# Weight rows on a 256-byte boundary in SBUF, and text V ahead of the scores, in a two-stream attention block

## Chip, cores, metric

One core of one Trainium2 chip. The metric is device time in microseconds (us) of one execution. Executions that are not over 1.5% above the fastest of the same kernel are called fast, the others slow. Ratios are of fast runs alone; medians and ranges take in all runs. SBUF is the core's on-chip memory, HBM the large memory from which the weights come; TensorE, VectorE (DVE in the lines) and ScalarE are engines of the core.

## The reference, cut to what matters

```python
B, Ni, Nt, D = (2, 256, 32, 1152)                     # bf16
mod_i = (silu(c) @ wmod_img).reshape(B, 6, 1, D)      # shift, scale, gate: blocks 0, 1, 2 (the rest unused)
hi = layernorm(x_img) * (1 + sci) + shi               # the same for the text stream
qi, ki, vi = split(hi @ wqkv_img)                     # and qt, kt, vt
p = softmax(concat(qt, qi) @ concat(kt, ki).T * D ** -0.5)
a = p @ concat(vt, vi)
out_i = x_img + gai * (ai @ wo_img)                   # and out_t
```

Fourteen weight blocks of 1152 x 1152 bf16 (2592 KB each) are used once each. Together with the inputs, and with the gate rows that the kernel writes out and reads back, they are 39.5 MB read from HBM.

## The kernel before

Five SBUF slots of 9 x 1152 bf16 per partition hold the weights. All loads go through one queue in the order of use; a load waits until the slot's last reader is done. A row of a weight block is 2304 bytes in one partition.

```python
const = ctx.enter_context(tc.tile_pool(name="const", bufs=1))
wpool = ctx.enter_context(tc.tile_pool(name="w", bufs=1))
act = ctx.enter_context(tc.tile_pool(name="act", bufs=1))
# ...
w_v_t = load_w(1, wqkv_txt, 2 * D)
w_ga_i = load_w(3, wmod_img, 2 * D)      # image gate
w_ga_t = load_w(2, wmod_txt, 2 * D)      # text gate
w_o_i = load_w(0, wo_img, 0)
w_o_t = load_w(1, wo_txt, 0)
# ... layer norm, V of the image, shift, Q and K of the image, the text's Q and K between them ...
def img_gate():
    mod_rows(w_ga_i, 1)                  # 36 matmuls on the gate's weights, copy, write to HBM
    for b in range(B):
        nc.gpsimd.dma_start(gb[:, b, :], gsc[1, b, :].partition_broadcast(P))
# ...
img_gate()
scores_txt()
scores_img(0)
scores_img(1)
v_txt()
p_transposes(0)
txt_gate()
attn_out(0, 0, 5)
# ... p_transposes(1), the rest of attention, then the four output tiles and the text's ...
```

Matmuls and the steps wrapped in `pin` keep the order in which they are written; other steps of VectorE and ScalarE may be reordered when the program is built.

## Time and profile before

| | before |
|---|---|
| median of 3 runs | 128.75 us (127.72 to 129.01) |
| span of the profiled execution | 127.2 us |
| TensorE busy | 116.3 us (91%) |
| weights streaming | about 3 to 103 us, at 390 GB/s |

The rows of busy tenths cut the span into 40 slices of 3.2 us; a 9 means 90% busy or more. PEclk is the granted clock of TensorE, in tenths of full speed. The view of waits says which engine waited, for whom, how long in all, how often, and the longest. The timeline gives start and duration of groups of instructions, with the idle time just before a group and what ended it in brackets. Those lines are in the prediction. One more place of this trace is needed later. VectorE, between the end of the scores and attention:

```profile
93.61 0.35 DVE L493 TENSOR_SCALAR pb<-e,rs 128x256 bf16<-128x256 f32 x1
93.88 0.23 DVE L495 TENSOR_SCALAR pb<-e,rs 128x32 bf16<-128x32 f32 x1
94.02 1.85 DVE L437 TENSOR_TENSOR v_t<-ps,svb 64x288 bf16<-64x288 f32 x4
95.91 0.61 DVE L535 COPY pT<-pT_ps 128x864 bf16<-128x864 bf16 x1
```

The last softmax tile (L493, L495) ends, then text V's four subtractions run, and only then comes the copy of P transposed that attention's first matmul needs.

### The profile page before, as it was taken

Reading aid. Unit: us, or ns where it says so; the run is one execution under the profiler, and the core shown is the slowest. Engines: PE = TensorE matmul, PEld = TensorE weight load, DVE = VectorE, ACT = ScalarE, POOL = GpSimd, SP = SyncE. Lnnn points to the kernel's source line nnn. Section 1 sums busy time; section 2 is a strip of 40 time slices with the busy share of each in tenths; the row PEclk is TensorE's granted clock in tenths of the full one; section 3 lists DMA queues with packets and bytes.
Section 4 is the critical chain, followed back from the end, with each engine's and each line's share of the span. In section 5 each row is a group of like instructions: output and inputs, shape, how many; then the busy total and the mean of one; then the engine's idle time right before and its main releaser. Section 6 shows DMA issues by size and latency. Waiting matters only on the chain.

```text
span 127.2 us, 2681 instructions
## 1 busy us (share of the span) xinstructions
PE 116.3 (91%) x1144; PEld 69.0 (54%) x1154; DVE 56.1 (44%) x151; ACT 34.1 (27%) x72; POOL 14.3 (11%) x36
## 2 busy tenths in 40 slices
PE   6998799999599999999999999669998999999990
PEld 2356644454176444545448466245786776566770
DVE  1576590067702732012261221204887565566672
ACT  4799400056511113211102011113513850000000
POOL 7230000000002133000000000003214171000000
PEclk9999999999999999999999999986999999999999
DMA  4999999999999999999999999999999992202212
GB/s 119 382 374 388 399 387 394 391 393 395 358 365 392 387 394 391 349 387 392 388 393 392 388 391 389 389 392 393 393 387 385 392 298 74 93 0 93 98 46 93
DMA packets 18694, 41.03 MB, mean 323 GB/s; under 512 B 1027, under 2 KB 1563, under 8 KB 18683
## 3 DMA queue, kind: packets, MB, share of 16 engines
q1 hardware_dynamic: 17584, 39.56, 84.4%
q0 software_dynamic: 704, 1.05, 2.5%
q10 hardware_dynamic: 395, 0.26, 0.7%
q8 instruction: 9, 0.15, 0.5%
q14 instruction: 2, 0.02, 0.0%
HBM read 39.52 MB, written 1.34 MB: 321 GB/s over the span
## 4 chain that ended last, share of the span: by engine, by line
PE 45%; DMA 36%; SPq 8%; DVE 6%; issue 1%; ACT 1%; DVEq 0%; ACTq 0%
PE ps L60 31%; DMA t<-in_wqkv_img_dram 18%; DMA t<-in_wmod_img_dram 18%; PE aps L60 5%; PE gps L60 4%; SPq L87 4%; PE sps L60 3%; SPq L101 2%; PE vps L60 2%; SPq L99 2%; DVE v_t L437 1%; ACT e L489 1%; DVE nmx L486 1%; DVE pb L493 1%; DVE pb L495 1%
## 5 line engine op out<-in xcount | busy, mean ns | idle before, releaser
L60 PE MATMUL ps<-xT_i,t 128*128 128x512 bf16 x156 | 35.5, 379 | 2.1 <-DMA t<-in_wqkv_img_dram 1.5
L60 PEld LDWEIGHTS <-t 128*128 128x128 bf16 x432 | 23.1, 97 | 20.7 <-DMA t<-in_wqkv_img_dram 2.0
L60 PE MATMUL ps<-t,aT 128*128 128x384 bf16 (+3 forms) x153 | 20.2, 308 | 0.0
L60 PEld LDWEIGHTS <-aT 128*128 128x128 bf16 (+1 forms) x153 | 13.0, 101 | 7.1 <-issue 0.5
L60 PE MATMUL vps<-t,hS_i 128*128 128x512 bf16 x70 | 15.9, 379 | 0.8 <-DVE hS_i L220 0.7
L60 PEld LDWEIGHTS <-hS_i 128*128 128x128 bf16 x72 | 6.9, 98 | 8.5 <-DVE hS_i L220 0.8
L60 PE MATMUL wps<-warm 128*128 128x512 bf16 x27 | 8.9, 486 | 1.3 <-DVE warm L119 1.2
L577 DVE TENSOR_TENSOR tmp<-ps,gb 128x384 bf16<-128x384 f32 (+2 forms) x13 | 6.8, 526 | 6.3 <-PE ps L60 6.3
L153 DVE CAST v_i<-vps 128x512 bf16<-128x512 f32 x5 | 3.4, 689 | 11.6 <-PE vps L60 11.6
L60 PE MATMUL gps<-t,sT 128*32 128x256 bf16 (+1 forms) x180 | 6.2, 281 | 2.5 <-DMA t<-in_wmod_img_dram 2.4
L155 ACT CAST qkT<-ps 128x512 bf16<-128x512 f32 (+1 forms) x6 | 3.4, 569 | 18.3 <-PE ps L60 18.3
L340 DVE TENSOR_SCALAR qkT<-ps 128x512 bf16<-128x512 f32 (+1 forms) x5 | 3.3, 665 | 10.6 <-PE ps L60 10.6
L153 DVE CAST qkT<-ps 128x512 bf16<-128x512 f32 (+1 forms) x5 | 3.1, 625 | 10.7 <-PE ps L60 10.6
L342 ACT ACTIVATE qkT<-ps 128x512 bf16<-128x512 f32 (+1 forms) x6 | 3.3, 553 | 15.9 <-PE ps L60 15.9
L60 PE MATMUL aps<-pT,v_i 128*128 128x288 bf16 x36 | 6.7, 287 | 0.5 <-DVE pT L535 0.5
L449 POOL DMA_DIRECT2D mod_scratch<-g_sb x4 | 2.3, 586 | 41.9 <-ACT g_sb L155 37.3
L60 PEld LDWEIGHTS <-sT 128*32 128x32 bf16 x180 | 4.5, 96 | 4.6 <-DMA t<-in_wmod_img_dram 2.9
L60 PE MATMUL sps<-qkT 128*128 128x288 bf16 (+1 forms) x54 | 6.9, 363 | 0.0
L549 DVE TENSOR_SCALAR aT<-aps,sv_i 128x288 bf16<-128x288 f32 x9 | 4.7, 517 | 3.0 <-PE aps L60 3.0
L551 ACT ACTIVATE aT<-aps,sv_i 128x288 bf16<-128x288 f32 x9 | 4.5, 501 | 5.4 <-PE aps L60 5.4
L60 PEld LDWEIGHTS <-warm 128*128 128x128 bf16 x29 | 3.1, 116 | 5.2 <-issue 2.7
L60 PEld LDWEIGHTS <-qkT 128*128 128x128 bf16 (+1 forms) x54 | 4.6, 120 | 2.1 <-issue 0.5
(100 smaller groups left out, 113.4 us busy)
## 6 DMA issues: line engine op xcount, KB each, us to landing
t<-in_wmod_txt_dram SPq DMA_DIRECT2D x3, 2592.0 KB, 21.2
t<-in_wqkv_txt_dram SPq DMA_DIRECT2D x3, 2592.0 KB, 16.2
t<-in_wmod_img_dram SPq DMA_DIRECT2D x2, 2592.0 KB, 21.8
t<-in_wqkv_img_dram SPq DMA_DIRECT2D x2, 2592.0 KB, 24.1
t<-in_wo_img_dram SPq DMA_DIRECT2D x1, 2592.0 KB, 21.3
t<-in_wo_txt_dram SPq DMA_DIRECT2D x1, 2592.0 KB, 12.2
t<-in_wmod_img_dram SPq DMA_DIRECT2D x2, 1152.0 KB, 9.5
t<-in_wqkv_img_dram SPq DMA_DIRECT2D x2, 864.0 KB, 15.2
```

What stands on the lines that cost most here:

```text
L60: return pin(nc.tensor.matmul(*a, **k))
L87: nc.sync.dma_start(t[:, :, o:o + n], sv[:, :, o:o + n])
L99: nc.sync.dma_start(w_sc_i[:, r0:r1, :], sc_v[:, r0:r1, :])
L101: nc.sync.dma_start(w_v_i[:, r0:r1, :], v_v[:, r0:r1, :])
L153: nc.vector.tensor_copy(out_ap, in_ap)
L155: nc.scalar.copy(out_ap, in_ap)
L340: nc.vector.tensor_scalar_mul(out_ap, in_ap, SCALE)
L342: nc.scalar.mul(out_ap, in_ap, SCALE)
L449: nc.gpsimd.dma_start(gsc[si, b, :].rearrange("(g j) -> g j", g=NGG), g_sb[b:P:32, :])
L549: nc.vector.tensor_scalar(dst, aps[:], bias, None, op0=ALU.add)
L551: nc.scalar.activation(dst, aps[:], ACT.Identity, bias=bias)
L577: nc.vector.tensor_mul(tmp[:, 0:n], ps[:, 0:n], gb[:, b, c0:c0 + n])
```

## The change

The intent is twofold: each weight row and input row shall begin on a 256-byte boundary of its partition, and TensorE shall have text V and half of the scores to do while the image gate's weights are still on their way.

```diff
-    const = ctx.enter_context(tc.tile_pool(name="const", bufs=1))
+    lead = ctx.enter_context(tc.tile_pool(name="lead", bufs=1))
     wpool = ctx.enter_context(tc.tile_pool(name="w", bufs=1))
     act = ctx.enter_context(tc.tile_pool(name="act", bufs=1))
+    const = ctx.enter_context(tc.tile_pool(name="const", bufs=1))
@@
+    eps_row = lead.tile([P, 32], f32)
@@
-    eps_t = const.tile([P, 1], f32)
-    nc.vector.memset(eps_t[:], EPS)
+    eps_t = eps_row[:, 0:1]
+    nc.vector.memset(eps_row[:], EPS)
@@
-    img_gate()
+    v_txt()
     scores_txt()
     scores_img(0)
+    img_gate()
     scores_img(1)
-    v_txt()
     p_transposes(0)
```

(Cut: the indexing of `eps_t` in one activation.)

More of the change, by code (lines that the diff above doesn't have):

```diff
@@ L179, in ln_rstd @@
         rstd = small.tile([P, 1], f32, tag="rstd")
-        pin(nc.scalar.activation(rstd[0:np_, :], var, ACT.Ln, bias=eps_t[0:np_, :], scale=sign))
+        pin(nc.scalar.activation(rstd[0:np_, :], var, ACT.Ln, bias=eps_t[0:np_], scale=sign))
         pin(nc.scalar.activation(rstd[0:np_, :], rstd[0:np_, :], ACT.Exp, scale=-0.5))
```

## The prediction

> **What bounds the kernel now.** I read the page's rows of busy tenths first, then the waits of TensorE, then the busy time by stretches, then the transfers. The rows:
>
> ```profile
> PE   6998799999599999999999999669998999999990
> ...
> PEclk9999999999999999999999999986999999999999
> DMA  4999999999999999999999999999999992202212
> GB/s 119 382 374 388 399 387 394 391 393 395 358 365 392 387 394 391 349 387 392 388 393 392 388 391 389 389 392 393 393 387 385 392 298 74 93 0 93 98 46 93
> ```
>
> Two resources are full at once. The DMA engines stream weights at about 390 GB/s from the second slice to about 103 us. TensorE is full but for two dents: slice 11 (about 33 us) and slices 26 and 27 (about 83 to 89 us), where the granted clock falls too. After 103 us there is only TensorE, VectorE and the tail. So what can be won is in the dents. The view of waits, for TensorE in all, names them:
>
> ```profile
> PE gps L60 <- DMA t<-in_wmod_img_dram: 2.4, 1, 2.4
> ...
> PE ps L60 <- DMA t<-in_wqkv_img_dram: 1.5, 1, 1.5
> ...
> PE aps L60 <- DVE pT L535: 0.5, 1, 0.5
> ```
>
> The first is the image gate's rows waiting for their weights; the second is the first Q block waiting for its weights; the third is attention waiting for the copy of P transposed. The timeline of TensorE gives the places:
>
> ```profile
> 30.06 3.18 PE L60 MATMUL vps<-t,hS_i 128*128 128x512 bf16 x14
> 34.74 2.12 PE L60 MATMUL ps<-xT_i,t 128*128 128x512 bf16 x9 [1.50 <-DMA t<-in_wqkv_img_dram]
> ...
> 79.80 1.67 PE L60 MATMUL ps<-xT_i,t 128*128 128x512 bf16 x7
> 83.90 1.40 PE L60 MATMUL gps<-t,sT 128*32 128x288 bf16 x36 [2.42 <-DMA t<-in_wmod_img_dram]
> 85.07 6.86 PE L60 MATMUL sps<-qkT 128*32 128x288 bf16 x54
> 91.86 2.40 PE L60 MATMUL ps<-t,hT_t 128*64 128x288 bf16 x36
> 94.19 0.68 PE L63 MATMUL pT_ps<-ident,pb 128*128 128x128 bf16 x9
> 94.80 1.29 PE L60 MATMUL gps<-t,sT 128*32 128x288 bf16 x36
> 96.57 0.42 PE L60 MATMUL aps<-pT,v_i 128*128 128x288 bf16 x2 [0.49 <-DVE pT L535]
> ```
>
> The columns are start, duration, engine, line, operation, count and, in brackets, the idle time before. Between 34.7 and 81.5 us there is no wait worth naming. The stretches around the second dent (us, then PE, PEld, DVE, ACT and POOL busy, the granted clock, DMA share and GB/s):
>
> ```profile
> 81.50:83.90 2.40, 0.00 (x1) 0.00 (x1) 0.69 (x1) 0.00 (x0) 0.00 (x0) 1.00 1.04 388
> 83.90:85.30 1.40, 1.40 (x40) 1.15 (x44) 0.00 (x0) 0.00 (x0) 0.00 (x0) 0.87 1.06 392
> 85.30:86.50 1.20, 1.20 (x19) 0.58 (x12) 0.00 (x0) 0.40 (x1) 0.47 (x1) 0.50 1.06 396
> 86.50:88.60 2.10, 2.10 (x11) 1.34 (x12) 0.90 (x2) 1.02 (x3) 0.69 (x2) 0.56 1.05 390
> 88.60:90.00 1.40, 1.40 (x14) 1.13 (x12) 1.26 (x6) 0.59 (x2) 0.00 (x0) 1.00 1.06 393
> ```
>
> The wait of 2.4 us is paid twice: it is followed by about 3.4 us at half clock. Lost there: 0.13 x 1.4 + 0.50 x 1.2 + 0.44 x 2.1 = 1.7 us. The dent therefore costs 2.4 + 1.7 = 4.1 us. The 1.5 us wait at 33 us is followed by no slow clock (1.00 throughout).
>
> [...]
>
> **Part 1, alignment.** As the kernel before is built, the 3232 B of the pool of constants come first, from byte 16512 of a partition, so the weight slots start at 19744 = 77 x 256 + 32. A row is 2304 B = 9 x 256, a slot 81 x 256, so every weight row, and every input row behind them, starts 32 B past a boundary and touches ten 256 B blocks. In the new layout one 128 B tile comes first: 16512 + 128 = 16640 = 65 x 256, and each row touches nine. At 391 GB/s a row takes 2304 x 16 / 391e9 = 94.3 ns[...]: 410 GB/s (5% more)[...]. The wider memset (128 x 32 for 128 x 1) is on VectorE at 0.8 us, under 0.1 us, before the input has landed: free.
>
> What a faster stream is worth is read where TensorE waits for it. The Q weights land at 34.7 us and streaming began at about 3 us. At 410 the 31.7 us become 31.7 x 391/410 = 30.2, so they land at 33.2. But TensorE ends its V work at 30.06 + 3.18 = 33.24 us, and its beginning hangs on the layer norm and the scale matmuls, which wait only 0.2 us for a DMA. So the win is **1.4 us, and can't be much over 1.5** however fast the stream becomes. Later landings move up by 3 to 5 us, but TensorE waits for none of them after part 2.
>
> **Part 2, order.** Nothing is added: text V (36 matmuls, 2.4 us), text scores and the scores of image 0 move ahead of the gate rows. Their operands are there: text V's weights lie one transfer ahead of the gate's in the queue, so land near 83.9 - 2654 KB / 390 GB/s = 77 us, and Q and K are in SBUF. From 81.5 us TensorE has 2.4 us of text V, about 0.7 of text scores and 2.2 of image 0 scores (18 matmuls; the last 27 of the 54 ran from 88.6 to 91.9 us at full clock, 0.12 us each), so reaches the gate near 86.8, 3 us after its weights are in at the old rate. The wait of 2.4 goes, and with it the half clock: **4.1 us**.
>
> Given back: the wait for P transposed. It was 0.5 us with text V between the scores and the transposes. Now only the transposes (0.68) and the text gate rows (about 1.25) lie between the end of the scores and attention, 1.9 us, against the last softmax (before, its last VectorE step ended at 94.1, 2.3 us after the scores) and 0.6 us for the copy: 2.9 - 1.9 = 1.0 us. So 0.5 us is added, perhaps less, as text V's four subtractions (1.85 us of VectorE just ahead of that copy) have gone earlier; I take **0.4**.
>
> The sum: 4.1 - 0.4 + 1.4 = 5.1 us. 128.75 - 5.1 = 123.65; I say 123.6.
>
> **Rivals.** First, a later transfer takes the wait's place. The text gate weights follow the image gate's by one transfer of 6.8 us: 90.7 at the old rate; the stretch from 83.9 to 96.57 us holds 12.7 - 1.7 - 0.5 = 10.5 us of work at full clock, the last 1.25 of it the text gate, so TensorE wants them near 81.5 + 10.5 - 1.25 = 90.7. A tie at the old rate, free at a better one. The image output weights land near 97.5 and are wanted near 100. The output weights for text, which in the kernel before are issued only at 94.3 us since they need text V's slot, are issued over 10 us earlier. Against it stand all these margins; it would cost 0 to 1 us.
>
> Second, the broadcast gate rows come late. The gate's rows are now made some 3 us later; before, 13.6 us lay between the end of the gate matmuls (85.3) and the second broadcast landing (91.98 + 6.9 = 98.9), with 6.6 us to spare before its first reader at 105.5. Now the rows end near 88.2, the broadcast lands near 101.8, and the first reader wants it near 101. A wait of about 1 us on VectorE is possible, but six PSUM buffers hold TensorE's output and VectorE needs only about 0.9 of each 1.46 us chunk: absorbed.
>
> Third, alignment does nothing, because reading HBM, and not writing SBUF, sets 390 GB/s. Then only part 2 counts: 128.75 - 3.7 = 125.05, or up to 126 with the first rival. The two parts overlap as well: a stream 5% faster would by itself bring the image gate's weights to about 79.9 us and remove most of that dent, so the parts are not worth their separate sums.
>
> Fourth, the half clock stays in part, from another short idle stretch: up to 1.7 us back, 125.3.
>
> **Range and chances.** The best case, all of the first dent and no added wait, is 128.75 - 5.7 = 123.05; the runs of the kernel before spread from 127.72 to 129.01, so I go to 122.2 below. Alignment without effect and a small new wait give 125.4 above. Faster by over 2% means under 126.2; even the order alone passes that by 1.1 us. Faster 0.93, same 0.06, slower 0.01.
>
> **What would show it.** Right: mean DMA rate from 10 to 30 us well above 393 GB/s; the idle before the first Q matmul near zero; no idle before the gate rows and a granted clock of 1.00 from 80 to 95 us; the wait before attention's first matmul 0.5 to 1.0 us; the stretch from the first output matmul to the end unchanged at about 23.4 us. Wrong: a rate still at 391, a new wait at the text gate or the first output chunk, or a clock dip that stays.

## The result, and the profile after

| | before | after |
|---|---|---|
| median | 128.88 us (127.72 to 129.38, 4 runs) | 123.27 us (123.15 to 124.34, 4 runs) |
| ratio of fast runs | | 0.9596 (0.9512 to 0.968) |
| span of the profiled execution | 127.2 us | 122.6 us |
| TensorE busy | 116.3 us | 116.0 us |

A ratio is the mean time of one kernel's fast runs over that of the other's fast runs of the same rounds, so it is not quite the ratio of the medians. The rows of the changed kernel:

```profile
PE   5977979999999999999999999999999999999990
...
PEclk9998699999999999999999999999999999999999
DMA  4999999999999999999999999999999950411222
GB/s 120 375 388 389 408 407 410 411 412 413 410 381 399 415 400 411 397 407 410 408 413 411 410 406 413 417 399 412 414 406 405 405 200 24 144 42 54 102 48 96
```

Both old dents of TensorE are gone, and from the fifth slice on the stream runs at 397 to 417 GB/s, with one slice at 381. There is a new spot: the granted clock falls in slices 4 and 5, from about 11 to 14.5 us (0.50 between 12 and 14 us). That belongs to this execution; the other three of the four had a mean clock of 1.00 and took 123.15 to 123.34 us, this one 124.34. The place of the second dent, in the timeline of TensorE:

```profile
77.25 4.05 PE L61 MATMUL ps<-xT_i,t 128*128 128x512 bf16 x18
81.23 2.40 PE L61 MATMUL ps<-t,hT_t 128*64 128x288 bf16 x36
83.55 3.10 PE L61 MATMUL sps<-qkT 128*32 128x288 bf16 x36
86.58 1.29 PE L61 MATMUL gps<-t,sT 128*32 128x288 bf16 x36
87.80 2.38 PE L61 MATMUL sps<-qkT 128*128 128x288 bf16 x18
90.02 0.67 PE L64 MATMUL pT_ps<-ident,pb 128*128 128x128 bf16 x9
90.61 1.29 PE L61 MATMUL gps<-t,sT 128*32 128x288 bf16 x36
91.91 0.42 PE L61 MATMUL aps<-pT,v_i 128*128 128x288 bf16 x2
```

Not one bracket: TensorE waits for nothing from Q to the end. Attention's first matmul starts at once too, where I expected a wait. VectorE shows why:

```profile
91.25 0.60 DVE L537 COPY pT<-pT_ps 128x864 bf16<-128x864 bf16 x1
91.77 0.15 DVE L493 RECIPROCAL rs<-rs 128x1 f32<-128x1 f32 x1
91.96 0.35 DVE L495 TENSOR_SCALAR pb<-e,rs 128x256 bf16<-128x256 f32 x1
```

The copy (L537) stands ahead of the last tile's reciprocal and products (from 91.77 us), though it is written after them. It serves the other image's attention and needs nothing from that tile.

### The profile page after: what moved, and what is told of

Read it like the earlier page. It is cut to its first block, busy times and chain, and to the rows that moved or that the text cites. A ratio compares the mean times of both kernels' runs of the same rounds, so it can differ in the third digit from the quotient of the medians.

```text
span 122.6 us, 2691 instructions
## 1 busy us (share of the span) xinstructions
PE 116.0 (95%) x1154; PEld 69.1 (56%) x1154; DVE 56.1 (46%) x151; ACT 34.2 (28%) x72; POOL 14.4 (12%) x36
## 4 chain that ended last, share of the span: by engine, by line
PE 88%; DMA 7%; DVE 1%; SPq 1%; issue 0%; DVEq 0%
PE ps L61 50%; PE vps L61 14%; DMA t<-in_wmod_img_dram 7%; PE gps L61 6%; PE aps L61 6%; PE sps L61 4%; PE tp L64 2%; PE sc_ps L61 2%; PE wps L61 2%; PE pT_ps L64 1%; SPq L97 1%; DVE tmp L579 1%; DVE o L580 0%; PE gT L64 0%; PE tpt L64 0%
## 5 line engine op out<-in xcount | busy, mean ns | idle before, releaser
L61 PE MATMUL ps<-xT_i,t 128*128 128x512 bf16 x162 | 36.5, 379 | 0.0
L157 ACT CAST v_i<-vps 128x512 bf16<-128x512 f32 x4 | 2.3, 580 | 12.3 <-PE vps L61 12.3
L61 PE MATMUL sps<-qkT 128*128 128x288 bf16 (+1 forms) x54 | 5.5, 287 | 0.0
```

Source lines behind the costliest of these rows:

```text
L61: return pin(nc.tensor.matmul(*a, **k))
L157: nc.scalar.copy(out_ap, in_ap)
```

## The experiments

The theory after the result has five points. The rate depends on how many 256-byte blocks a row touches in SBUF (ten in the kernel before, at 392 GB/s from 20 to 30 us, nine in the changed one, at 412). A faster stream is worth 1.4 us at the first Q matmul. Either part of the change alone removes most of the wait for the gate's weights. The half clock comes from that wait. The wait for P transposed fell away through VectorE's order. All results were correct save the one that is wrong on purpose. The runs called slow, which the ratios leave out, are one of copy_last, one of before_again, and 4 of the 27, 1 of the 11 and 4 of the 18 runs of the kernel before.

| run | median us (range, runs) | before in the same rounds | ratio of fast runs |
|---|---|---|---|
| align_only | 124.04 (123.88 to 124.75, 6) | 127.88 (27) | 0.9684 |
| order_only | 124.55 (124.36 to 125.04, 6) | the same | 0.9720 |
| after_again | 123.20 (122.89 to 124.14, 6) | the same | 0.9623 |
| before_filled | 127.77 (127.48 to 128.45, 22) | the same | 0.9999 |
| offset_128 | 124.45 (124.32 to 124.64, 4) | 128.62 (11) | 0.9703 |
| offset_224 | 124.75 (124.43 to 125.06, 4) | the same | 0.9722 |
| source_32 | 122.72 (122.60 to 122.81, 4) | the same | 0.9564 |
| copy_last | 124.26 (124.04 to 126.96, 6, one slow) | the same | 0.9691 |
| before_again | 127.78 (127.18 to 129.29, 14) | 127.97 (18) | 0.9997 |
| after_third | 123.41 (123.04 to 123.90, 5) | the same | 0.9655 |
| start_filled | 123.34 (123.25 to 123.38, 4) | the same | 0.9651 |
| before_third | 127.62 (one look) | 128.61 (1) | |

### Each part alone: align_only, order_only, after_again

```diff
 align_only: the new pools, and the old order
+    img_gate(); scores_txt(); scores_img(0); scores_img(1); v_txt(); p_transposes(0)
 order_only: the old pools, and the new order
+    v_txt(); scores_txt(); scores_img(0); img_gate(); scores_img(1); p_transposes(0)
 after_again: the changed kernel, unedited
```

> The new layout with the old order of work. Theory (the two parts mend the same dent): the DMA rate is 405 to 412 GB/s as in the changed kernel, Q's weights land near 33.3 us, and the image gate's weights land near 80.4 us, when TensorE is ready for them near 79.9, so the wait of 2.4 us shrinks to 0.5 or less and no half clock follows it. The 0.5 us wait for P transposed stays. Expected 124.1 us (123.4 to 125.0), that is within 1 us of the changed kernel. Rival (each part has its own gain, alignment only that of Q's weights): 127.4 us.

> The new order with the old layout, rows 32 bytes past a boundary. Theory: the rate stays at 391 GB/s, the 1.5 us wait for Q's weights stays, the wait before the gate rows and the half clock go, and no wait for P transposed appears: 128.9 - 4.1 - 0.5 = 124.3 us (123.8 to 125.3). Rival (the text gate's or the output weights arrive too late at the old rate): a new wait of 0.5 to 1.5 us, 125.0 to 126.0. Rival (additive parts): what alignment did not give, 128.9 - 4.0 = 124.9, which this run cannot tell from the theory; the run of alignment alone can.

> The changed kernel again, for its times on the same chip as the three others. 123.2 us in runs without a slow clock in the start, some 124.3 in runs with one.

Alignment alone gave 124.04 us (124.1 expected, 127.4 by the rival). Its timeline at the two dents:

```profile
29.87 3.19 PE L61 MATMUL vps<-t,hS_i 128*128 128x512 bf16 x14
33.51 2.12 PE L61 MATMUL ps<-xT_i,t 128*128 128x512 bf16 x9 [0.46 <-DMA t<-in_wqkv_img_dram]
...
80.54 1.29 PE L61 MATMUL gps<-t,sT 128*32 128x288 bf16 x36 [0.28 <-DMA t<-in_wmod_img_dram]
81.65 5.30 PE L61 MATMUL sps<-qkT 128*32 128x288 bf16 x54
...
92.05 0.42 PE L61 MATMUL aps<-pT,v_i 128*128 128x288 bf16 x2 [0.95 <-DVE pT L537]
```

The wait for the gate's weights shrank to 0.28 us without any reordering. The wait for P transposed, of which I had expected that it stays at 0.5 us, was 0.95. So the parts are not additive: alone they are worth 3.2% and 2.8%, together 3.8%. The intervals of these ratios overlap, since the kernel before spreads so much; the runs themselves show it better: all of align_only took 123.88 us or more, all of order_only 124.36 or more, and five of the six of after_again 123.58 or less. The order alone gave 124.55 us (124.3 expected) and kept its 1.60 us wait for Q's weights. From order_only to after_again alignment is worth 124.55 - 123.20 = 1.35 us. In after_again the first Q matmul started at 33.12 us, and its last short wait was no longer for a DMA:

```profile
29.66 3.18 PE L61 MATMUL vps<-t,hS_i 128*128 128x512 bf16 x14
33.12 2.12 PE L61 MATMUL ps<-xT_i,t 128*128 128x512 bf16 x9 [0.28 <-DVE xT_i L323]
```

So there is a cap on what a faster stream can give there: VectorE's modulation of the input is the next limit. It lies close: in align_only Q still waited for its weights, 0.46 us, in start_filled 0.35, and in source_32 for VectorE again. From align_only to after_again the order is worth 0.84 us; the two waits that it removes, 0.95 us for P transposed and 0.28 for the gate, would make 1.2.

### Which bytes and which side: offset_128, offset_224, source_32

```diff
 offset_128, on the changed kernel
-    eps_row = lead.tile([P, 32], f32)
+    eps_row = lead.tile([P, 64], f32)
 offset_224
+    eps_row = lead.tile([P, 88], f32)
 source_32 (wrong result on purpose)
     def wview(src, c0):
+        if src.shape[1] > D:
+            c0 += 16 if c0 == 0 else -16
```

> The changed kernel with the leading tile 256 bytes wide in place of 128, so that every weight row starts 128 bytes past a 256-byte boundary. Theory [...]: the rate from 20 to 30 us is 391 GB/s as at offset 32, and the time is that of the order alone, 124.5 us. Rival (what counts is a boundary of 64 or 128 bytes): 410 to 412 GB/s and 123.2 us. [...]

> The same with a leading tile of 352 bytes, rows 224 bytes past a boundary. Theory of blocks: 391 GB/s again, 124.5 us. Rival of 64-byte boundaries: 391 here too but 411 at offset 128. [...]

> Wrong result on purpose: SBUF rows stay on the boundary, and the twelve loads from the wide weights read columns shifted by 16 elements, so that each row in HBM starts 32 bytes past a boundary or before one. Theory (what costs is the write into SBUF): 408 to 412 GB/s from 20 to 30 us and 123.2 us. Rival (the read [...] costs the same): 391 GB/s and 124.5 us.

The start of each row in SBUF was read from the programs as built: 32 bytes past a 256-byte boundary before, 0 in the changed kernel, 128 and 224 in these two. Busy times, granted clock, DMA share and GB/s from 20 to 30 us. Before:

```profile
20.00:30.00 10.00, 9.79 (x84) 4.91 (x85) 2.78 (x6) 1.91 (x4) 0.00 (x0) 1.00 1.05 392
```

The changed kernel:

```profile
20.00:30.00 10.00, 10.00 (x72) 4.73 (x73) 2.83 (x7) 1.76 (x3) 0.00 (x0) 1.00 1.04 412
```

offset_128:

```profile
20.00:30.00 10.00, 9.61 (x86) 4.86 (x85) 2.87 (x6) 2.00 (x4) 0.00 (x0) 1.00 1.05 391
```

offset_224:

```profile
20.00:30.00 10.00, 10.00 (x79) 4.79 (x76) 2.63 (x6) 1.76 (x3) 0.00 (x0) 1.00 1.05 391
```

source_32, aligned in SBUF and shifted in HBM:

```profile
20.00:30.00 10.00, 10.00 (x88) 4.94 (x86) 3.23 (x9) 2.56 (x5) 0.00 (x0) 1.00 1.04 412
```

The last column decides: 391 or 392 at offsets 32, 128 and 224, and 412 at 0, with the source rows in place and with them shifted by 32 bytes. Neither the size of the offset nor a boundary of 64 or 128 bytes matters in these runs, and the shift on the read side doesn't either. What the three slow layouts share is one more 256-byte block per row in SBUF, and with it two blocks that a row fills in part only. No run tells these two apart; rows whose length is no multiple of 256 bytes would. The times agree: 124.45 and 124.75 us, as with the order alone. That source_32 is some 0.5 us quicker than the changed kernel in other rounds is not explained; the changed kernel did not run in its rounds.

### Does the idle time cause the half clock: before_filled, before_again, before_third

```diff
 before_filled, on the kernel before, ahead of img_gate()
+    fps = ps_tr.tile([P, 512], f32, tag="tr")
+    for _ in range(11):
+        mm(fps[:], lhsT=warm[:, 0:P], rhs=warm[:], start=True, stop=True)
 before_again, before_third: the kernel before, unedited
```

> The kernel before with eleven matmuls of 128x512 on a zero tile ahead of the image gate's rows (11 x 0.216 = 2.4 us of work that nobody reads), so that TensorE is busy while it waits for the gate's weights. Theory (the half clock comes from the idle 2.4 us): the granted clock stays at 1.00 from 80 to 95 us and the kernel wins the 1.7 us lost at half clock: 127.2 us (126.7 to 127.8). Rival (the slow clock has another cause, such as the load of the work there): the dip stays and the time is 128.9 or more.

> The kernel before, for a second trace. Theory (the half clock behind the wait for the gate's weights comes in some executions only[...]): its runs fall in two groups, near 127.4 us and near 128.9 us, and a trace of the first group shows the same wait of about 2.4 us with a granted clock of 1.00 behind it. Rival (the wait itself is shorter in the faster executions): a wait near 1 us there.

> The kernel before, one more look, for a trace of its quicker group of executions (mean clock 1.00 or a dip in the start only, span near 125.6 us), which fell in about 6 of 10. Theory: the wait for the gate's weights is 2.0 to 2.5 us as in the slower group, and no half clock follows it, so the 54 matmuls of the scores take 5.3 us in place of 6.9. Rival: the wait is near 1 us there. If the trace falls in the slower group, this stays open.

before_filled missed its number: I expected 127.2 and it took 127.77, the same as the kernel before in its rounds. The clock came as expected, the size did not. Its trace has a granted clock of 1.00 from 80 to 94 us, and its scores took 5.30 us in place of 6.86:

```profile
84.15 1.29 PE L60 MATMUL gps<-t,sT 128*32 128x288 bf16 x36 [0.32 <-DMA t<-in_wmod_img_dram]
85.27 5.30 PE L60 MATMUL sps<-qkT 128*32 128x288 bf16 x54
```

But the kernel before was not what I had taken it for. Of its 27 runs in those rounds 16 took 127.14 to 128.03 us, and 11 took 128.31 to 129.33, all of these at a mean clock of 0.987 or less. (The mean clock alone does not tell the groups apart: seven of the 16 have 0.984 to 0.986, so a slow stretch somewhere. In the last rounds the groups run into each other.) The profiled execution that I had predicted from was one of the second kind. before_again, with 9 runs at 127.18 to 128.11 and 5 at 128.45 to 129.29, was profiled in that kind too: after a wait of only 2.10 us its scores took 6.90 us. before_third is of the first kind, at a mean clock of 1.00:

```profile
83.69 1.29 PE L60 MATMUL gps<-t,sT 128*32 128x288 bf16 x36 [2.19 <-DMA t<-in_wmod_img_dram]
84.80 5.30 PE L60 MATMUL sps<-qkT 128*32 128x288 bf16 x54
90.03 2.40 PE L60 MATMUL ps<-t,hT_t 128*64 128x288 bf16 x36
...
95.21 0.42 PE L60 MATMUL aps<-pT,v_i 128*128 128x288 bf16 x2 [0.96 <-DVE pT L535]
```

Nearly the same wait, 2.19 us, the scores at full clock in 5.30 us, and a wait for P transposed of 0.96 us in place of 0.49. So half clock followed an idle stretch of this length in some executions only (2.42 us in before and 2.10 in before_again, not 2.19 in before_third), and where it did, half of a microsecond came back, because the slower TensorE waited less for VectorE (0.49 and 0.47 us against 0.96). The net cost of the dip is (6.86 - 5.30) + (1.40 - 1.29) - (0.96 - 0.49) = 1.2 us; the spans differ by 127.2 - 125.8 = 1.4. before_filled has 0.95 us before attention as well, which leaves it no gain over the quicker group (in its trace the gate's weights landed at 84.1 us, 0.3 us after the fill's end, and the gate rows waited for them). What it did gain is steadiness: none of its 22 runs was above 128.45, where 10 of the 27 were. That, and not its one trace, which looks like before_third's, is the evidence that the idle time causes the half clock.

Why only in some executions? No run shows it. The clock records of two traces show this much: the slow stretch in before and the one in the changed kernel's first profile last 3.41 us each, and the full-speed stretches ahead of them are whole multiples of that, 78.51 us or 23 times in before, 6.83 us or twice in the changed kernel. The length of the wait alone does not tell the executions apart, as 2.10 us had half clock behind it and 2.19 us did not; and no run moved the wait against the clock's changes.

### The order on VectorE: copy_last

```diff
 copy_last, on the changed kernel
+    last = pin if key == (B - 1, TPB - 1) else (lambda i: i)
+    last(nc.vector.reciprocal(...)); last(nc.vector.tensor_scalar_mul(...))   # the last tile's steps
-    nc.vector.tensor_copy(pT[:], pT_ps[:])
+    pin(nc.vector.tensor_copy(pT[:], pT_ps[:]))
```

> The changed kernel with VectorE's steps of the last softmax tile and its copy of P transposed held in the order in which they are written, so that the copy comes after the last tile. In the changed kernel the copy was issued ahead of that tile's last three steps and attention did not wait. Theory (that is why the wait I predicted did not come): attention's first matmul now waits 0.6 to 1.1 us for the copy, and the time is 0.6 to 1.1 us longer, 124.1 us. Rival (there is slack anyway): no wait, 123.2 us.

It took 124.26 us, 1.0 us more than the changed kernel elsewhere; by the ratios, 0.9691 against 0.9623 and 0.9655, the loss is 0.4 to 0.7%, so 0.5 to 0.9 us. Its profile fell in a slow execution (125.2 us of span, a mean clock of 0.983, and a wait of 2.0 us for Q's weights), so I take from it the order alone: the copy comes at 93.87 us, straight after the last tile's products at 93.73, and attention's first matmul waits 1.0 us:

```profile
94.53 0.42 PE L61 MATMUL aps<-pT,v_i 128*128 128x288 bf16 x2 [1.02 <-DVE pT L538]
```

The sign is shown by the fast runs (124.04 us at least; 12 of the changed kernel's 15 runs took 123.58 or less). The exact size is not, as the changed kernel was not in those rounds.

### The start: start_filled, after_third

```diff
 start_filled, on the changed kernel
-    warm_up(15)
+    warm_up(17)
@@
     x_transposes(3, 0)()
+    warm_up(2)
     sc_cols(0, 4)
```

> The changed kernel with two more warm-up matmuls before the first transposes and two before the first scale matmuls, where TensorE was idle 0.8 and 0.7 us in the execution that then ran from 11 to 14.5 us at half clock. Theory: no execution has that dip, so none is above 123.8 us, and the median stays at 123.2, since the Q weights' landing near 33.3 us still sets when TensorE goes on. Rival (the extra matmuls are themselves on the path): 0.3 to 0.9 us slower.

> The changed kernel, to be compared with the next one in the same rounds: 123.2 us, and 124.2 in the executions with a slow clock in the start.

In the changed kernel's first profile TensorE idled 0.76 us before the first transposes and 0.69 us before the first scale matmuls, and ran at half clock (0.50) from about 11 to 14.5 us. Q then started at 34.57 us in place of 33.12. after_third's profile had the dip too (mean clock of 0.66 from 10 to 15 us, after waits of 0.7 and 0.5 us). Over all 15 runs of the changed kernel, 3 are of this kind (two of them profiled, the third by its mean clock of 0.986), at 123.90 to 124.34 us. None of start_filled's four runs is above 123.38, but four runs can't show that a dip of one run in five is gone, and its median is the same. It is no version that is shown to beat the change; I leave it open.

In the kernel before such a dip in the start cost nothing: before_filled's profile has one (half clock from 12.0 to 15.4 us) and its Q still started at 34.73 us, as before at 34.74, since Q's weights came no earlier.

## Why the prediction was right

- **The stream.** 410 GB/s was predicted, 412 measured. The cause, rows that start on a 256-byte boundary of SBUF, is what the offsets show; whether by one block less or by none filled in part, they don't. The size was a guess of mine that came out; no trace had shown it. At 391 GB/s a row takes 94.3 ns and at 412 it takes 2304 x 16 / 412e9 = 89.5 ns, 4.8 ns less. Nor did the 5.1 us hang on the exact rate: by the prediction's own cap of about 1.5 us at Q, any rate from 410 up gives nearly the same.
- **The first Q matmul.** 1.4 us predicted, 1.35 measured between order_only and after_again, with a cap about where it was said to be: Q started at 33.12 us, 0.28 us after TensorE's V work, held there by VectorE, which the prediction had not named.
- **The gate's wait.** It went, and its weights were in SBUF in time. The text gate and the output weights caused no new wait, in order_only at the old rate neither. The broadcast gate rows did, as the second rival said ("A wait of about 1 us on VectorE is possible"): not in the first profile, which the dip in the start had delayed, but by 1.08 us in after_again and 2.5 in order_only:

```profile
99.50 0.56 DVE L579 TENSOR_TENSOR tmp<-ps,gb 128x384 bf16<-128x384 f32 x1 [1.08 <-DMA gb<-mod_scratch]
```

It was absorbed, as said: from the first output matmul to the end it is 122.6 - 99.14 = 23.5 us in the first profile, 121.1 - 97.70 = 23.4 in after_again and 122.7 - 99.32 = 23.4 in order_only.

- **The half clock: the term that was mis-sized.** I charged "4.1 us" for the dent, 1.7 of it for the half clock, as if each execution paid it. In the rounds with 27 runs of the kernel before, 11 have the time of one that paid, and the net cost is some 1.2 us, since 0.5 us less was then lost at P transposed. The profile of one execution can't tell this; the spread of 127.72 to 129.01 us in the three times I had was the hint, and I read it as noise. (A small misreading besides: TensorE's dent is in slices 26 and 27, 79.5 to 85.9 us, and the clock's in 27 and 28, 82.7 to 89.0; the prediction gives both as 26 and 27.)
- **P transposed: the step that failed.** The prediction says "So 0.5 us is added, perhaps less" and takes 0.4. The wait vanished: a gain of 0.5 us against the slower executions of the kernel before and 0.95 against the quicker. I had placed the copy behind the last softmax tile, as it is written; it was issued ahead of it. The sum itself was sound: copy_last, which forces the order that I had assumed, waits 1.02 us, where the prediction has 1.0. What failed was the assumed order of VectorE's steps, which are not pinned.
- **The sum.** 5.1 us predicted, 128.88 - 123.27 = 5.6 found. The two errors have opposite signs, so that the sum came this near is in part luck. Against the quicker group of the kernel before (16 of the 27 runs, median 127.55 us), the gain is 4.35 us: 2.2 for the gate's wait, 0.95 for P transposed and 1.35 for Q make 4.5. In two more sets of rounds the ratio was 0.9623 and 0.9655. The gain is nearer to these 3.5 to 3.8% than to the 4.0% of the first four runs, of which three of the kernel before were slower ones.
- **The rivals.** "The two parts overlap as well" was right: alignment alone left 0.28 us of the gate's wait.

## What to carry to other kernels

Where weight rows are streamed into SBUF, look at the byte at which the first weight tile lands in its partition: a few constants allocated ahead of it put every row off the boundary and cost this stream of 2304-byte rows 5% of its rate (391 GB/s against 412; other lengths were not run). A faster stream is worth only what the first engine that waits for it can use before its next limit, so read the gain there and not from the total. When two changes mend the same wait, measure each alone, and when the times of a kernel form two groups, find out which group the profile came from before charging a term to it.
